# Attention, dense FFN and expert FFN in one kernel: values of eight heads in one part, space of its own for the first expert tile, two gather buffers

## The chip, the cores and the metric

The kernel runs on one core of a Trainium2 chip. The metric is the device time of one execution in microseconds (us). The profile names the engines PE (TensorE), DVE (VectorE), ACT (ScalarE), POOL (GpSimd) and SP (SyncE); PEld is the weight load of PE.

## The reference

Three layers follow each other: a linear attention with complex decay, a dense FFN, and an expert FFN that sends each token to one of eight experts.

```python
# attention: q, k, v, a of [4, 8, 768, 48]; scale a to magnitude <= 0.999
for t in range(S):
    S_re, S_im = ar * S_re - ai * S_im, ar * S_im + ai * S_re
    S_re = S_re + k[t] (x) v[t]
    y[t] = q[t] @ S_re
x = y as [3072, 384]
# dense FFN, 384 -> 2048 -> 384
h = x @ w_in
x = (h * tanh(log1p(exp(h)))) @ w_out
# experts, 8 of 384 -> 1024 -> 384
logits = x @ w_gate + modality_bias[modality_id]
e = argmax(logits); gate = softmax(logits)[e]
out = gate * (relu(x @ w1[e]) @ w2[e])
```

All is float32. The kernel gets float32 accuracy from products of three matmuls on values split into a high and a low half (`xh`/`xl`, `gh`/`gl`, `hhs`/`hls`, `v` in sets of two).

## The kernel before

**Work.** 3072 tokens are cut into 12 units of 256. A unit goes through the attention in two chunks of 128 tokens (`scores`, a mask on DVE, `values` into `py`, the carried state `st`), then through the dense FFN in 8 steps. An h step (`ph`) has 18 matmuls, and its o step (`po`, 12 matmuls) follows three steps later (LAG = 3). The last o step of a unit gives the gate logits; routing sorts the tokens of a half of the sequence into expert tiles: `route 0` for the first half runs during the later units, `route 1` for the second half after the last unit, in some 125 small DVE instructions on the scratch `ar`, whose result is `tt` (which rows to fetch and where to put them). Tiles 0 to 4 hold the first half's tokens, 5 to 11 the second half's, 256 rows each; 12 to 14 are small tiles of 128 rows.

**A tile.** Four loads of 768 KB bring the weights of its expert into `r0s`/`r1s`; ACT writes the high half and DVE the low half (`v`, 128x1536). POOL gathers the rows by an indirect DMA (`xg`), PE transposes them (`pt`), ACT and DVE split them into `y`. Then four steps of `qhs` (18 matmuls) and `qos` (12), again with a lag of three, and a scatter of the results (`out<-oss`, POOL). In a small tile one `qhs` has 9 matmuls of 512 columns.

**What sets the order.** Class `Plan` (L91) collects strands: lists of operations with a due time. `run` lists them out greedily, at each step the operation that can start first by modelled costs, on a tie the one with the earlier due time. What `part()` encloses stays together on one engine; `wait` and `mark` name events, and a mark of kind "order" counts from the issue of the instruction before it. The emitted order is fixed at build time: on each engine instructions run in that order, and semaphores make them wait for data. Nearly all work is recorded through one helper, so that its line in the profile is L261. Class `Line` keeps the PE steps of FFN and tiles in one chain: step n's h matmuls, then the o matmuls of step n-3, or in the other order where `swap` is set. `NoStep` is an empty step in that chain.

**Names that the change touches.** `att_scores` (L541) issues scores, masks and values of a chunk. Each tile gets its transposed rows from `Tile.rows` (L1350), which waits in the strand `gather n` for the routing and for the transposes of the tile before (`tu{n-1}`), because there is one buffer `xr` for the gathered rows. Tile 0's rows `y` lie in the buffers `xh` and `xl` of the dense FFN, and wait for the h matmuls of the last step (`H95`). `g.const` is a pool that lives to the end, `g.stk` a pool of the attention that is freed behind it.

Of the kernel before, what the change touches and what calls it, by code (L numbers as in the profile page):

```python
# [7 lines left out]
F32 = mybir.dt.float32  # L8
F32R = mybir.dt.float32r
I32 = mybir.dt.int32  # L10
# [6 lines left out]
B, H, S, D = 4, 8, 768, 48  # L17
DM = H * D
NT = B * S
DFF = 2048  # L20
E, F2 = 8, 1024
CH = 128
NU = NT // 256
KD = DM // 128
# [260 lines left out]
def setup(g, ins):  # L285
    nc = g.nc
    c = g.const
    g.ident = c.tile([128, 128], F32, name="ident")
    g.mask = c.tile([128, 1, 128], F32, name="mask")
    nc.sync.dma_start(out=g.ident, in_=ins["c_ident"])  # L290
    nc.sync.dma_start(out=g.mask[:, 0, :], in_=ins["c_mask"])
    g.nident = c.tile([128, 128], F32R, name="nident")
    nc.scalar.activation(out=g.nident, in_=g.ident, func=AF.Copy, scale=-1.0)
    nc.scalar.preload_act_table_set("natural_log_exp_and_others")
    for t in g.vt + g.st:
        nc.gpsimd.memset(t[:, :, 48:64], 0.0)
    for t, n in zip(g.scan, (1, 2, 4, 1)):
        nc.gpsimd.memset(t[:, 0, 0:n], 1.0)
        nc.gpsimd.memset(t[:, 1, 0:n], 0.0)
    g.dend = c.tile([128, NU, 6], F32, name="dend")  # L300
    g.asum = c.tile([128, NU + 1], F32, name="asum")
# [239 lines left out]
def att_scores(g, ins, ci, xT):  # L541
    nc, p = g.nc, g.plan
    u, c = divmod(ci, 2)
    cc = ci % 6
    QK, v, s0 = g.QK[u], g.vt[ci % 2], g.st[ci % 2]
    p.wait(f"QK{u}_0")
    py = g.aps.tile([128, 4, 128], F32, tag="py", name=f"py{ci}")
    sc = {}

    def scores(hg):  # L550
        ps = g.aps.tile([128, 4, 128], F32, tag="ps", name=f"ps{ci}_{hg}")
        with p.part():
            for h in range(4):
                nc.tensor.matmul(ps[:, h, :], QK[hg][0:96, h, 1, c, 0:128], QK[hg][0:96, h, 0, c, 0:128], start=True, stop=True)
        return ps

    def mask(hg, ps):
        sc[hg] = g.apw.tile([128, 4, 128], F32, tag="sc", name=f"sc{ci}_{hg}")
        nc.vector.tensor_mul(sc[hg], ps, g.mask.to_broadcast([128, 4, 128]))

    def values(hg):
        with p.part():
            for h in range(4):
                hh = hg * 4 + h
                o = py[(hh % 2) * 64:(hh % 2) * 64 + 64, hh // 2, :]
                nc.tensor.matmul(o, v[:, hh, :], sc[hg][:, h, :], start=True, stop=cc == 0)
                if cc > 0:
                    nc.tensor.matmul(o, s0[:, hh, :], QK[hg][0:96, h, 0, c, 0:128], start=False, stop=True)

    mask(0, scores(0))  # L570
    p.wait(f"QK{u}_1", f"v{ci}")
    ps = scores(1)
    if cc > 0:
        p.wait(f"s{ci - 1}")
    values(0)
    mask(1, ps)
    values(1)
    p.mark(f"y{ci}")
    Y = g.apw.tile([128, 4, 128], F32, tag="sc", name=f"Y{ci}")
    nc.scalar.copy(out=Y, in_=py)  # L580
    dst = xT.rearrange("(p a e) t -> a e p t", a=2, e=48)
    for a in range(2):
        with p.behind(f"x{u}"):
            nc.sync.dma_start(out=dst[a, :, :, ci * 128:(ci + 1) * 128], in_=Y[a * 64:a * 64 + 48])
# [339 lines left out]
def route_setup(g, ctx, ins):  # L924
    nc = g.nc
    c = g.const
    g.iota_e = c.tile([128, 1, E], F32, name="iota_e")
    g.iota_t = c.tile([128, NHALF[1], 1], F32, name="iota_t")
    g.iota_p = c.tile([128, 128], F32, name="iota_p")
    g.ids = c.tile([128, NT // 128, 2], F32, name="ids")  # L930
    g.tri = c.tile([128, 128], F32, name="tri")
    g.ones = c.tile([128, 128], F32, name="ones")
    nc.sync.dma_start(out=g.iota_e[:, 0, :], in_=ins["c_iota_e"])
    nc.sync.dma_start(out=g.iota_t[:, :, 0], in_=ins["c_iota_t"])
    nc.sync.dma_start(out=g.iota_p, in_=ins["c_iota_p"])
    nc.sync.dma_start(out=g.ids, in_=ins["c_ids"])
    nc.sync.dma_start(out=g.tri, in_=ins["c_tri"])
    nc.vector.memset(g.ones, 1.0)
    route_space(g, c)
    g.etab = [c.tile([128, NFM + NSM + 2], I32, name=f"etab{i}") for i in range(2)]  # L940
    g.bias = c.tile([128, NT // 128, E], F32, name="bias")
    mb = c.tile([128, 2, E], F32, name="mb")
    mi = c.tile([128, NT // 128, 2], I32, name="mi")
    nc.sync.dma_start(out=mb, in_=ins["mb"].partition_broadcast(128))
    nc.sync.dma_start(out=mi, in_=ins["mid"].bitcast(I32).rearrange("p (b w) -> p b w", w=2))
    sh = [128, NT // 128, E]
    m0 = c.tile([128, NT // 128], F32, name="m0")
    m1 = g.logit
    V = nc.vector
    V.tensor_scalar(out=m0, in0=mi[:, :, 0], scalar1=0.0, scalar2=None, op0=ALU.is_equal)  # L950
    V.tensor_mul(g.bias, m0.unsqueeze(2).to_broadcast(sh), mb[:, 0:1, :].to_broadcast(sh))
    V.tensor_scalar(out=m0, in0=mi[:, :, 0], scalar1=1.0, scalar2=None, op0=ALU.is_equal)
    V.tensor_mul(m1, m0.unsqueeze(2).to_broadcast(sh), mb[:, 1:2, :].to_broadcast(sh))
    V.tensor_add(g.bias, g.bias, m1)
# [340 lines left out]
class Tile:  # L1295


    def __init__(self, g, ins, n, gi, i, halves, x2, out):
        self.g, self.n, self.gi, self.i, self.halves, self.out = g, n, gi, i, halves, out
        at = 2 * i if halves == 2 else 2 * NFM + i  # L1300
        self.tt = g.tt[gi][:, :, at:at + halves]
        self.w1, self.w2 = g.sets[n % 2]
        self.hs, self.ph, self.po = {}, {}, None
        self.due = due(NU) + min(n, NA + NB) * TSTEP * 4 + max(n - NA - NB, 0) * TSTEP * 1.5
        self.nm = f"s{n}"
        if n == 0:
            self.x = [g.mx.tile([128, KD, 256], F32R, tag=t, name=f"y{t}", bufs=1) for t in ("xh", "xl")]
        else:
            self.x = g.xsets[n % 2]
        self.weights(ins)  # L1310
        self.rows(x2)
# [39 lines left out]
    def rows(self, x2):  # L1351
        g, p, n, tt = self.g, self.g.plan, self.n, self.tt
        nc = p
        nr = NT * (self.gi + 1) // 2
        xg = g.mx.tile([128, 2, DM], F32, tag="xr", name=f"xg{n}", bufs=1)
        pts = []
        with p.strand(f"gather {n}", self.due - 30), p.behind(f"G{n}"):
            p.wait(f"tt{self.gi}", *(f"x2_{b}" for b in range(nr // 128)), f"tu{n - 1}" if n else f"X{NU - 1}")
            for c in range(self.halves):
                p.gpsimd.indirect_dma_start(  # L1360
                    out=xg[:, c], out_offset=None, in_=x2[0:nr, :],
                    in_offset=bass.IndirectOffsetOnAxis(ap=tt[:, 0, c:c + 1].bitcast(U32), axis=0),
                    bounds_check=nr - 1, oob_is_err=False)
        with p.strand(f"turn {n}", self.due - 12):
            p.wait(f"G{n}")
            for c in range(self.halves):
                p.take("pt")
                pt = g.m2.ps.tile([128, KD, 128], F32, tag="pt", name=f"pt{n}_{c}")
                with p.part():
                    for k in range(KD):  # L1370
                        p.tensor.transpose(pt[:, k, :], xg[:, c, k * 128:(k + 1) * 128], g.ident)
                pts.append(pt)
                p.mark(f"pt{n}_{c}")
            p.mark(f"tu{n}")
        xh, xl = self.x
        for c in range(self.halves):
            with p.strand(f"rows {n} {c}", self.due - 11):
                p.wait(f"pt{n}_{c}")
                if n == 0:
                    p.wait(f"H{8 * NU - 1}")  # L1380
                elif n == 1:
                    p.wait(f"O{8 * NU - 5}")
                elif n == 2:
                    p.wait(f"O{8 * NU - 7}")
                if n > 2:
                    p.wait(*self.tiles[n - 2].done(1))
                cs = slice(c * 128, (c + 1) * 128)
                split(g, xh[:, :, cs], xl[:, :, cs], pts[c])
                p.give("pt")
                p.mark(f"Y{n}")  # L1390
# [30 lines left out]
class TileStep:  # L1421
    middle = None

    def __init__(self, tile, j):
        self.t, self.j = tile, j
        self.due = tile.due + j * TSTEP
        self.swap = tile.n == j == 0

    def first(self, line):
        t, j = self.t, self.j  # L1430
# [234 lines left out]
def body(tc, ctx, ins, out):  # L1665
# [34 lines left out]
    moe2_sets(g)  # L1700
    w1 = g.wts.tile([128, WP[1]], F32, tag="w9", name="ar1")
    Tile.tiles = tiles = []
    steps.extend([NoStep] * 2)
    for n in range(NA + NB + NS):
        gi, i, halves = (0, n, 2) if n < NA else (1, n - NA, 2) if n < NA + NB else (1, n - NA - NB, 1)
        tiles.append(Tile(g, ins, n, gi, i, halves, x2, out))
# [101 lines left out]
```

## Time and profile before

| | |
|---|---|
| median of 3 runs | 955.14 us (952.89 to 955.41) |
| profiled execution | 951.5 us, span 949.6 us |
| PE busy | 874.9 us, 92% of the span |
| DVE busy | 732.7 us, 77% |
| ACT busy | 668.8 us, 70% |
| POOL busy | 175.2 us, 18% |

The span is the time from the first to the last instruction of the profiled execution. Busy shares are means over stages: the attention starts up to about 125 us, attention and dense FFN run side by side to about 670, the expert tiles follow up to about 936, and the last scatters end the span. A time in brackets behind a row is how long the engine was idle before it, and the arrow names what ended that.

### The profile page before, as it was taken

Reading aid. Unit: us, or ns where it says so; the run is one execution under the profiler, and the core shown is the slowest. Engines: PE = TensorE matmul, PEld = TensorE weight load, DVE = VectorE, ACT = ScalarE, POOL = GpSimd, SP = SyncE. Lnnn points to the kernel's source line nnn. Section 1 sums busy time; section 2 is a strip of 40 time slices with the busy share of each in tenths; the row PEclk is TensorE's granted clock in tenths of the full one; section 3 lists DMA queues with packets and bytes.
Section 4 is the critical chain, followed back from the end, with each engine's and each line's share of the span. In section 5 each row is a group of like instructions: output and inputs, shape, how many; then the busy total and the mean of one; then the engine's idle time right before and its main releaser. Section 6 shows DMA issues by size and latency. Waiting matters only on the chain.

```text
span 949.6 us, 17369 instructions
## 1 busy us (share of the span) xinstructions
PE 874.9 (92%) x6401; PEld 828.8 (87%) x6401; DVE 732.7 (77%) x1517; ACT 668.8 (70%) x1093; POOL 175.2 (18%) x237
## 2 busy tenths in 40 slices
PE   1489899999999999998999999999899999999993
PEld 1267789999999989998999999999799999999883
DVE  4989788889898988798889899764699865565541
ACT  5786969787968787887788787767754556556551
POOL 1021202112120221030303020202112034332211
PEclk9979899999999999999999999999799999999997
DMA  9923323425252534233524142305654767666730
GB/s 306 347 68 89 96 71 113 112 78 124 78 124 67 135 93 109 68 95 107 134 68 123 46 102 67 93 26 194 225 190 136 247 216 237 218 223 212 235 123 7
DMA packets 102749, 128.22 MB, mean 135 GB/s; under 512 B 34601, under 2 KB 76599, under 8 KB 102656
## 3 DMA queue, kind: packets, MB, share of 16 engines
q1 hardware_dynamic: 89680, 89.00, 31.4%
q0 software_dynamic: 12976, 38.03, 13.3%
q8 instruction: 52, 0.85, 0.4%
q14 instruction: 41, 0.34, 0.1%
HBM read 93.74 MB, written 14.82 MB: 114 GB/s over the span
## 4 chain that ended last, share of the span: by engine, by line
PE 46%; ACT 22%; issue 11%; DMA 9%; DVE 8%; POOL 2%; SPq 0%; ACTq 0%; POOLq 0%; DVEq 0%
PE ph L261 11%; PE po L261 10%; ACT u L261 9%; PE py L261 5%; PE ps L261 5%; DMA out<-oss,tt 5%; PE qhs L261 4%; ACT X L261 3%; ACT S L261 3%; PE pst L261 3%; PE qos L261 3%; PE pl L261 2%; DVE ar L261 1%; ACT gh L261 1%; ACT v L261 1%
## 5 line engine op out<-in xcount | busy, mean ns | idle before, releaser
L261 ACT ACTIVATE u<-u 128x512 f32<-128x512 f32 x384 | 237.8, 629 | 6.5
L261 PE MATMUL po<-wt,gh 128*128 128x392 f32 x768 | 206.7, 350 | 2.3 <-ACT gh L261 2.0
L261 PE MATMUL ph<-xh,wt 128*128 128x256 f32 x1152 | 193.5, 288 | 6.6 <-ACT xh L261 4.1
L261 PEld LDWEIGHTS ph<-xh,wt 128*128 128x128 f32 x1152 | 163.5, 191 | 11.5 <-ACT xh L261 4.8
L261 PEld LDWEIGHTS po<-wt,gh 128*128 128x128 f32 x768 | 135.2, 190 | 6.6 <-issue 2.9
L261 PE MATMUL po<-wt,gl 128*128 128x392 f32 x384 | 132.0, 344 | 2.1 <-DVE gl L261 2.1
L261 PE MATMUL qos<-v,hhs 128*128 128x384 f32 x432 | 111.8, 339 | 0.0
L261 POOL DMA_DIRECT2D QK<-X x120 | 65.6, 554 | 230.7 <-ACT xs L261 72.1
L261 PE MATMUL qhs<-y,v 128*128 128x256 f32 x792 | 103.1, 283 | 0.0
L261 PE MATMUL ph<-xl,wt 128*128 128x256 f32 x576 | 101.5, 285 | 1.6 <-DVE xl L261 1.4
L261 PEld LDWEIGHTS qhs<-y,v 128*128 128x128 f32 x792 | 98.7, 189 | 0.0
L261 DVE TENSOR_TENSOR v<-r1s,v 128x1536 fp32r<-128x1536 f32 x30 | 52.7, 1757 | 49.0 <-ACT v L261 46.1
L261 ACT ACTIVATE u<-ph 128x512 f32<-128x512 f32 x96 | 56.7, 591 | 45.6 <-PE ph L261 41.9
L261 DVE SCALAR_TENSOR_TENSOR u<-u,ph 128x512 f32<-128x512 f32 x96 | 65.5, 683 | 26.3 <-ACT u L261 26.1
L261 PEld LDWEIGHTS ph<-xl,wt 128*128 128x128 f32 x576 | 82.7, 191 | 3.2 <-DVE xl L261 3.1
L261 DVE TENSOR_TENSOR gl<-u,gh 128x512 fp32r<-128x512 f32 x96 | 65.7, 686 | 14.6 <-ACT gh L261 14.5
L261 ACT ACTIVATE gh<-u 128x512 fp32r<-128x512 f32 x96 | 60.1, 627 | 23.7 <-DVE u L261 23.6
L261 PEld LDWEIGHTS po<-wt,gl 128*128 128x128 f32 x384 | 72.9, 190 | 3.5 <-DVE gl L261 3.3
L261 PEld LDWEIGHTS qos<-v,hhs 128*128 128x128 f32 x432 | 75.3, 188 | 0.1
L261 POOL DMA_INDIRECT xg<-x,tt x27 | 42.3, 1568 | 167.5 <-PE pt L261 116.6
L261 PE MATMUL qos<-v,hls 128*128 128x384 f32 x216 | 72.6, 336 | 0.0
L261 ACT ACTIVATE hhs<-qhs 128x512 fp32r<-128x512 f32 x48 | 28.7, 599 | 59.2 <-PE qhs L261 58.2
(149 smaller groups left out, 1598.3 us busy)
## 6 DMA issues: line engine op xcount, KB each, us to landing
r0s<-in_w SPq DMA_DIRECT2D x30, 768.0 KB, 4.5
r1s<-in_w SPq DMA_DIRECT2D x30, 768.0 KB, 4.8
QK<-X POOLq DMA_DIRECT2D x72, 96.8 KB, 3.4
QK<-X SPq DMA_DIRECT2D x72, 96.8 KB, 3.7
r<-in_wo SPq DMA_DIRECT2D x8, 768.0 KB, 7.9
r<-in_wi SPq DMA_DIRECT2D x8, 768.0 KB, 13.5
X<-in_q POOLq DMA_DIRECT2D x12, 384.0 KB, 4.9
A<-in_ai POOLq DMA_DIRECT2D x12, 384.0 KB, 4.5
```

Source lines behind the costliest of these rows:

```text
L261: self.plan.add(self.name, *cost[:2], lambda: real(*a, **k), *cost[2:])
```

## The change

`values` of both groups of four heads are issued in one part, behind both masks. Four small tiles (`mask`, `mb`, `mi`, `m0`) move from the pool that lives to the end to that of the attention. Tile 0's rows get space of their own (`yh`, `yl`) and no longer wait for the last h step; its first `qhs` follows in the usual order of a step, and the two empty steps ahead of it go. The gathered rows lie in two buffers: odd tiles from 3 on take the buffer `xh`, so that gather n waits for the transposes of tile n-2 (gather 3 for the last h step), and an order mark `gg` keeps the gathers in sequence.

```diff
 def att_scores
     mask(0, scores(0))
     p.wait(f"QK{u}_1", f"v{ci}")
-    ps = scores(1)
+    mask(1, scores(1))
     if cc > 0:
         p.wait(f"s{ci - 1}")
-    values(0)
-    mask(1, ps)
-    values(1)
+    with p.part():
+        values(0)
+        values(1)
...
-    g.mask = c.tile([128, 1, 128], F32, name="mask")
+    g.mask = g.stk.tile([128, 1, 128], F32, name="mask")
...
         if n == 0:
-            self.x = [g.mx.tile([128, KD, 256], F32R, tag=t, name=f"y{t}", bufs=1) for t in ("xh", "xl")]
+            self.x = [g.m2.w.tile([128, KD, 256], F32R, name=f"y{t}") for t in "hl"]
...
-        xg = g.mx.tile([128, 2, DM], F32, tag="xr", name=f"xg{n}", bufs=1)
+        xg = g.mx.tile([128, 2, DM], F32, tag="xh" if n > 2 and n % 2 else "xr", name=f"xg{n}", bufs=1)
+        behind = f"H{8 * NU - 1}" if n == 3 else f"tu{n - 2 + (n < 3)}" if n else f"X{NU - 1}"
...
-            p.wait(f"tt{self.gi}", *(f"x2_{b}" for b in range(nr // 128)), f"tu{n - 1}" if n else f"X{NU - 1}")
+            p.wait(f"tt{self.gi}", *(f"x2_{b}" for b in range(nr // 128)), behind, *([f"gg{n - 1}"] if n else []))
...
+            p.mark(f"gg{n}", "order")
...
-                if n == 0:
-                    p.wait(f"H{8 * NU - 1}")
-                elif n == 1:
+                if n == 1:
                     p.wait(f"O{8 * NU - 5}")
...
-        self.swap = tile.n == j == 0
+        self.swap = False
...
-    steps.extend([NoStep] * 2)
```

**In the instruction order, PE at the start of unit 7.** `py_481` are the values of that unit's second chunk, `ph_6` and `ph_7` the last h steps of the unit before; `ph_0` of unit 7 follows behind two more o steps in both. The end of the values before:

```order
L261 MATMUL py_481<-QK_7_464,st_98 64x128
L261 MATMUL py_481<-sc_1_485,vt_96 64x128
L261 MATMUL py_481<-QK_7_464,st_98 64x128
L261 MATMUL ph_7_892<-xh_858,wt_252 128x256 x3
L261 MATMUL ph_7_892<-xl_859,wt_252 128x256 x3
L261 MATMUL ph_7_892<-xh_858,wt_252 128x256 x3
L261 MATMUL po_0_878<-wt_217,gh_4_883 128x392 x2
```

With the change the last rows of `py` and what stands next to them:

```order
L261 MATMUL py_481<-QK_7_464,st_98 64x128
L261 MATMUL py_481<-sc_1_485,vt_96 64x128
L261 MATMUL py_481<-QK_7_464,st_98 64x128
L261 MATMUL ph_6_888<-xh_858,wt_239 128x256 x3
L261 MATMUL ph_6_888<-xl_859,wt_239 128x256 x3
L261 MATMUL ph_6_888<-xh_858,wt_239 128x256 x3
L261 MATMUL po_0_878<-wt_204,gh_3_877 128x392 x2
```

The values have moved from the middle of `ph_7` into `ph_6`: half an h step, an o step and half an h step stand between more than before.

**PE at the change of stage.** `po` with `wt_230` is o step 5 of the last unit, `wt_243` o step 6; `pt_0` and `pt_1` are transposes of tile 1's rows. Before:

```order
L261 MATMUL po_1_1074<-wt_230,gh_5_7513 128x392 x2
L261 MATMUL po_1_1074<-wt_230,gl_5_7512 128x392
L261 MATMUL pt_0_7413<-ident,xg_7412 128x128 x3
L261 MATMUL pt_1_7414<-ident,xg_7412 128x128 x3
L261 MATMUL po_0_1073<-wt_243,gh_6_7517 128x392 x2
L261 MATMUL po_0_1073<-wt_243,gl_6_7516 128x392
```

With the change, from the end of o step 4 (`wt_217`):

```order
L261 MATMUL po_1_1074<-wt_217,gl_4_1077 128x392
L261 MATMUL qhs_0_7522<-yh,v_0_7378 128x256 x3
L261 MATMUL qhs_0_7522<-yl,v_0_7378 128x256 x3
L261 MATMUL qhs_0_7522<-yh,v_2_7380 128x256 x3
L261 MATMUL qhs_0_7522<-yh,v_0_7378 128x256 x3
L261 MATMUL qhs_0_7522<-yl,v_0_7378 128x256 x3
L261 MATMUL qhs_0_7522<-yh,v_2_7380 128x256 x3
L261 MATMUL po_0_1073<-wt_230,gh_5_7513 128x392 x2
```

`qhs_0` of tile 0 stands between o steps 4 and 5 now, and `qhs_1` to `qhs_3` in the same way behind 5, 6 and 7.

**POOL at the last tiles.** `xg_7489`, `xg_7495` and `xg_7501` are the gathers of tiles 12, 13 and 14; the `out` rows come in pairs, one pair to a tile of 256 rows. Before:

```order
L261 DMA out<-oss_0_7675,tt_618 3072x384
L261 DMA out<-oss_1_7676,tt_618 3072x384
L261 DMA xg_7489<-x_61,tt_618 128x384
L261 DMA out<-oss_0_7691,tt_618 3072x384
L261 DMA out<-oss_1_7692,tt_618 3072x384
L261 DMA xg_7495<-x_61,tt_618 128x384
L261 DMA out<-oss_0_7707,tt_618 3072x384
L261 DMA out<-oss_1_7708,tt_618 3072x384
L261 DMA xg_7501<-x_61,tt_618 128x384
L261 DMA out<-oss_0_7726,tt_618 3072x384
```

With the change:

```order
L261 DMA xg_7489<-x_61,tt_618 128x384
L261 DMA out<-oss_0_7675,tt_618 3072x384
L261 DMA out<-oss_1_7676,tt_618 3072x384
L261 DMA xg_7495<-x_61,tt_618 128x384
L261 DMA out<-oss_0_7691,tt_618 3072x384
L261 DMA out<-oss_1_7692,tt_618 3072x384
L261 DMA xg_7501<-x_61,tt_618 128x384
L261 DMA out<-oss_0_7707,tt_618 3072x384
L261 DMA out<-oss_1_7708,tt_618 3072x384
L261 DMA out<-oss_0_7726,tt_618 3072x384
```

Each gather stands one pair of scatters further ahead.

## Rows read from the trace of the kernel before

**Rows 1.** Windows: start:end, length, busy us (instructions) by engine, PEclk, DMA share, GB/s.

```profile
0.00:75.00 75.00, 39.69 (x185) 28.78 (x185) 57.60 (x104) 54.10 (x90) 10.08 (x31) 0.91 0.67 229
125.00:650.00 525.00, 514.93 (x4034) 493.27 (x4034) 445.35 (x1032) 411.98 (x726) 83.38 (x140) 1.00 0.36 98
440.00:450.00 10.00, 7.52 (x45) 7.23 (x46) 8.18 (x11) 9.90 (x15) 0.00 (x0) 0.83 0.30 90
676.00:684.00 8.00, 5.85 (x18) 4.81 (x18) 5.18 (x7) 4.29 (x6) 0.25 (x1) 0.50 0.91 325
684.00:759.30 75.30, 75.15 (x552) 74.84 (x552) 67.95 (x171) 38.52 (x45) 11.25 (x10) 1.00 0.61 192
700.00:895.00 195.00, 193.90 (x1396) 192.88 (x1395) 135.09 (x220) 108.06 (x131) 56.08 (x41) 1.00 0.67 213
```

**Rows 2.** Timeline of PE, starts of units 5 and 7: start, us, operation [idle before].

```profile
334.05 0.44 PE L261 MATMUL py<-QK,st 96*64 96x128 f32 x4
...
343.54 0.62 PE L261 MATMUL ph<-xh,wt 128*128 128x256 f32 x3 [1.36 <-ACT xh L261]
...
433.52 0.44 PE L261 MATMUL py<-QK,st 96*64 96x128 f32 x4
...
442.26 0.92 PE L261 MATMUL ph<-xh,wt 128*128 128x256 f32 x3 [2.75 <-ACT xh L261]
```

**Rows 3.** Timeline of PE, end of the last unit and start of tile 0.

```profile
667.97 0.52 PE L261 MATMUL po<-wt,gh 128*128 128x392 f32 x2
...
671.74 0.63 PE L261 MATMUL po<-wt,gh 128*128 128x392 f32 x2 [0.72 <-ACT gh L261]
673.62 0.45 PE L261 MATMUL po<-wt,gl 128*128 128x392 f32 x1 [1.25 <-DVE gl L261]
...
677.84 1.02 PE L261 MATMUL po<-wt,gh 128*128 128x392 f32 x2 [1.30 <-ACT gh L261]
679.72 0.69 PE L261 MATMUL po<-wt,gl 128*128 128x392 f32 x1 [0.85 <-DVE gl L261]
...
692.49 0.52 PE L261 MATMUL qos<-v,hhs 128*128 128x384 f32 x2
```

**Rows 4.** Timeline of ACT in the same stretch.

```profile
677.71 1.48 ACT L261 ACTIVATE v<-r1s 128x1536 fp32r<-128x1536 f32 x1
...
688.37 0.60 ACT L261 ACTIVATE hhs<-qhs 128x512 fp32r<-128x512 f32 x1 [1.56 <-PE qhs L261]
```

**Rows 5.** Tile 5: DVE's group of hls before tt, then timelines of DVE, POOL, PE.

```profile
L261 DVE SCALAR_TENSOR_TENSOR hls<-qhs,hhs 128x512 fp32r<-128x512 f32 x17 | 11.6, 685 | 1.7 <-ACT hhs L261 1.7
...
759.26 0.20 DVE L261 CAST tt<-tb 128x38 int32<-128x38 f32 x1 [1.26 <-PE tb L261]
...
759.58 1.75 DVE L261 TENSOR_TENSOR v<-r1s,v 128x1536 fp32r<-128x1536 f32 x1
...
759.73 2.52 POOL L261 DMA_INDIRECT xg<-x,tt  x1 [7.27 <-DVE tt L261]
...
766.55 1.03 PE L261 MATMUL pt<-ident,xg 128*128 128x128 f32 x6 [0.95 <-DMA xg<-x,tt]
...
772.69 2.28 PE L261 MATMUL qhs<-y,v 128*128 128x256 f32 x18
```

**Rows 6.** Tile 14: timeline of POOL, then of PE.

```profile
887.41 1.05 POOL L261 DMA_INDIRECT xg<-x,tt  x1 [8.58 <-PE pt L261]
...
895.42 0.98 POOL L261 DMA_INDIRECT out<-oss,tt  x1 [3.18 <-ACT y L261]
896.71 2.18 POOL L261 DMA_INDIRECT xg<-x,tt  x1 [0.30 <-issue]
...
903.52 0.88 PE L261 MATMUL pt<-ident,xg 128*128 128x128 f32 x3 [3.43 <-DMA xg<-x,tt]
904.05 3.50 PE L261 MATMUL qhs<-v,y 128*128 128x512 f32 x9
...
909.93 2.25 PE L261 MATMUL qhs<-v,y 128*128 128x512 f32 x9
```

More of the change, by code (lines that the diff above doesn't have):

```diff
@@ L561, in values @@
     def values(hg):
[L562 to L568, printed above, removed]
+        for h in range(4):
+            hh = hg * 4 + h
+            o = py[(hh % 2) * 64:(hh % 2) * 64 + 64, hh // 2, :]
+            nc.tensor.matmul(o, v[:, hh, :], sc[hg][:, h, :], start=True, stop=cc == 0)
+            if cc > 0:
+                nc.tensor.matmul(o, s0[:, hh, :], QK[hg][0:96, h, 0, c, 0:128], start=False, stop=True)
     mask(0, scores(0))
     p.wait(f"QK{u}_1", f"v{ci}")
-    ps = scores(1)
+    mask(1, scores(1))
     if cc > 0:
         p.wait(f"s{ci - 1}")
-    values(0)
-    mask(1, ps)
-    values(1)
+    with p.part():
+        values(0)
+        values(1)
     p.mark(f"y{ci}")
@@ L941, in route_setup @@
     g.bias = c.tile([128, NT // 128, E], F32, name="bias")
-    mb = c.tile([128, 2, E], F32, name="mb")
-    mi = c.tile([128, NT // 128, 2], I32, name="mi")
+    mb = g.stk.tile([128, 2, E], F32, name="mb")
+    mi = g.stk.tile([128, NT // 128, 2], I32, name="mi")
     nc.sync.dma_start(out=mb, in_=ins["mb"].partition_broadcast(128))
@@ L946, in route_setup @@
     sh = [128, NT // 128, E]
-    m0 = c.tile([128, NT // 128], F32, name="m0")
+    m0 = g.stk.tile([128, NT // 128], F32, name="m0")
     m1 = g.logit
```

## The prediction

> **What bounds the kernel now.** I read the table of windows first [rows 1]. From 125 to 650 us TensorE (PE) is busy in 514.93 of 525 us, from 700 to 895 in 193.90 of 195, both at the full granted clock: there only fewer or shorter pauses of PE can shorten the kernel, and a pause saved ahead of 700 us reaches the end. PE is idle at the start (39.69 of 75 us busy), at the change from the dense FFN to the expert tiles around 676, and behind its last matmul, where the change moves nothing. So I looked next at PE's timeline for every wait over 0.2 us: four places stay, and the change touches each.
>
> First, starts of units [rows 2]. A unit's first h step needs the attention output of its tokens, which goes through a copy on ScalarE, two DMAs and a split. At unit 7 the last `py` ends at 433.96 and the first `ph` begins at 442.26, 8.3 us later, 2.75 of them a wait; at unit 5 it is 334.49 to 343.54, 9.05 us, with 1.36 of wait. After unit 7's wait the granted clock of 440 to 450 is 0.83 [rows 1], between the levels of 1.2 and 2.4 GHz: of 7.52 busy us some 17% or 1.3 us are lost. Second, the change of stage [rows 3]: o steps 6 and 7 of the last unit wait 0.72, 1.25, 1.30 and 0.85 us, 4.12 together, and the clock is 0.50 between 676 and 684. Third, tile 5: its gather starts when the routing of the second half is done (`tt` at 759.26), and its transposes wait 0.95 us for `xg` [rows 5]. Fourth, tile 14: its transposes wait 3.43 us for `xg`, and then comes a `qhs` group of 3.50 us where the next takes 2.25 [rows 6].
>
> **Values of eight heads in one part.** The 8 or 16 small matmuls no longer stand in two places. Work is the same. They stand behind both masks now, and the scheduler, which gives a part to PE without a gap, places the last `py` elsewhere between the steps. A step of 18 `qhs` matmuls takes 2.28 us [rows 5]; an o step has 12 of 392 columns, 2% more columns in all; I count 2.2 for each kind. By the order of before, 3.5 steps stood between the last `py` and the first `ph` of unit 5 (7.7 us) and 2.5 at unit 7 (5.5 us), against a chain of 8.3 to 9.05: short by 1.4 and 2.8 to 3.5, as the waits say. All other units had 4.5 steps (9.9 us) or more and no wait. By the order of after it is 4 steps (8.8) at units 2, 5 and 8, 3.75 (8.2) at 11, and 4.5 or more at all others, 7 among them. Removed: 1.36 + 2.75 + 1.3 = 5.4 us. Added: 8.7 (middle of the two chains) less the cover is 0 at 2, 5 and 8 and 0.5 at 11; with the longer chain 0.25 three times and 0.85, with half a clock loss 1.4 in the middle. Taken: -4.0; bounds -5.4 (no new wait) and 0 (chain at its longest and a clock loss of 1.3 at three of the four places, 1.6 + 3.9 = 5.5). The wait for the second mask costs PE nothing as long as a step stands between; the order keeps one there. The start, 0 to 75 us, is ordered a little differently as well: PE is no bound there (39.69 busy) and DVE with 57.60 does the same work: 0, bounds -3 and +3, about the size of one unit-start wait.
>
> **Tile 0 with its own space.** Before, tile 0's rows took the `xh` and `xl` buffers of the last unit, so its first step came after all of that unit's h steps and two empty steps kept the lag. Now `qhs` 0 to 3 stand between o steps 4 to 7. PE's work from the start of o step 5 at 667.97 to the first `qos` at 692.49 [rows 3] is the same: three o steps (6.6), four `qhs` groups (9.1), six transposes (1.0), 16.7 of 24.5 us at the full clock. At most 7.8 us can go. What is late next is ScalarE: `gh` of step 7 came at 677.84, and now two `hhs` (0.60 each) and one `v` (1.48) more stand ahead of it [rows 4], 2.7 us: 680.5. From there o step 7 and `qhs` 3 take 4.4 us, so `qos` starts at 684.9: -7.6. Lower bound -7.8; upper -3, if `gh` comes later by two more splits (3.0) and PE's clock falls again. The moves of the mask and bias tiles to another pool issue the same DMAs: nothing.
>
> **Tile 5 behind it.** PE now reaches tile 5 7.6 us earlier, 772.69 - 7.6 = 765.1. Its rows come from `tt`: `tt` 759.26, transposes 766.55, hence 7.3 us, then 2.7 for the transposes and the two splits: `tt` + 10. DVE works through `tt`'s small operations among weight splits; from 684 to 759.3 it is busy 67.95 of 75.30 us [rows 1]. In the new order 14 instead of 17 `hls` of 685 ns stand ahead of it, -2.1 us; its start is 1 us later (a split more ahead); of 7.35 us of idle time between none or half goes. `tt` falls between 758.2 and 754.5, and tile 5 between 768.2 and 764.5, a loss of 3.1 or of 0. I take +1.0. If the routing is no faster at all it is 769.3, +4.2.
>
> The descriptor instruction of that gather takes 2.52 us beside a `v` split on DVE that runs from 759.58 to 761.33 [rows 5], while the scatter's at 895.42, with no such split, takes 0.98 [rows 6]. The Trainium skill (SBUF — State Buffer, section "SBUF: two separate sides") states that GpSimd is locked out of the port it shares with DVE, and cannot write descriptors, while DVE runs a two-port operation. The trace agrees at this place: the instruction ends 0.9 us after the split. By that rule, an estimate, an earlier gather gains or loses up to 1.5 us by what DVE does just then; by the rows alone I add nothing for it.
>
> **Two gather buffers.** A gather of tile n now waits for the transposes of tile n-2. Only two gathers are late in the trace, those of tiles 5 and 14; the others have landed when PE comes, so their earlier start is worth nothing. Tile 14's was issued at 896.71, behind the `out` scatter of 895.42 [rows 6], and PE waited 3.43 us. Its new condition, the transposes of tile 12, was met when tile 13's gather was issued at 887.41, and it stands ahead of that scatter pair now, so up to 9.3 us earlier: it lands near 894, when PE wants it near 900. -3.43, and -1.25 for the slow group after it: -4.7. Bounds: -5.1 (the three transposes too, 0.88 us where six took 1.03 [rows 5]) and 0 (the gather late still, held by what is queued ahead on POOL). What is queued behind these gathers on POOL are scatters of tiles done, for which nobody waits but the last one; that one is unchanged, and so is the tail after PE's end. The further wait that tile 0's rows lose (for the last h step) is in the 7.6.
>
> **Sum.** -4.0 - 7.6 + 1.0 - 4.7 = -15.3 us. The profiled execution took 951.5 us (span 949.6 and 1.9 around it): 936.2. It was 3.6 us faster than the median of the runs shown, 955.14, so the median after is 955.1 - 15.3 = 939.8; I say 940.
>
> **Rivals.**
> (A) The second routing sets tile 5. DVE, not PE, is then the bound from 684 to 769: the whole of what the change of stage gives but 3.4 us is given back as a wait of `pt` for `xg` at tile 5. For it: DVE's 67.95 of 75.30 us. Against: three `hls` less, and idle time that can go. -4.0 - 7.6 + 4.2 - 4.7 = -12.1, 943; with `tt` 3 us later still, 946.
> (B) The unit starts gain nothing: the chain is longer than 9 us at units with 4 steps of cover, or the start loses 3 us. For it: four units are within 0.9 us of the chain. Against: units with 9.9 us did not wait. -11.3 to -8.3, 944 to 947.
> (C) Slower. The chain from the last `py` to `xh` grows at most units, for one cause: the values wait for both masks and the state, so the copy behind them lands among other ScalarE work, 2 us later or more. Each hit costs what unit 7 cost, 2.75 + 1.3 = 4.05 us. The rest gains 11.3, the two old hits return, so with three more hits the gain is gone (12.2), and with six more it is 955.1 - 11.3 + 24.3 = 968. For it: the new covers lie between 8.2 and 9.9, nearer to the chain than most of before. Against: the chain was 8.3 to 9.05 where it could be read, and one wait on a mask (beside a 2.2 us step) is short.
> (D) It doesn't do what it says: `qhs` 0 to 3 stand early but wait for the `v` splits of tile 0, which now compete with the last unit's `gh` and `gl`, and PE waits in another place, at half clock, for as long as before. The stage's change then gives 0. With unit starts and tail as forecast that is -8.7, 946; with the tail's gather late still 951, and with the unit starts at their upper bound too 955, no change.
>
> **How the numbers follow.** Forecast 0.52 (its own range 935 to 944), A 0.18 (943 to 946), B 0.13 (944 to 947), D 0.09 (946 to 955, 0.04 of it above 952.2), C 0.08 (from four hits, 960). A measurement of this kernel tells about 0.3%, 2.9 us, from no change. Faster: 0.52 + 0.18 + 0.13 + 0.05 = 0.88; same 0.04; slower 0.08. The range 932 to 950 leaves out C, the worse half of D and a little below: 2 in 10 at most. Its low end is -23, which takes every lower bound (-5.4, -3 at the start, -7.8, 0, -5.1: -21.3) and 1.5 for the run.
>
> **What would show it.** Values: no wait over 0.6 us of `ph` on `xh` at unit starts but at 2, 5, 8 or 11; wrong if units with 4.5 steps wait over 1 us. Transition: first `qos` near 685 less what the units saved, clock above 0.9 from 670 on, and under 1.5 us of waits. Tile 5: `pt<-ident,xg` waits under 1 us and `tt` lies some 70 us behind the last `logit`; if that wait is 3 us or more it is A. Tail: no wait on `xg` in the last small tile and `qhs` at 2.25 us. The prediction is wrong if PE shows a wait on something that was on no row of before: above all on `v`, `y` or `sc`.

## The result: 932.5 us, 22 us faster, at the lower end of the range

The changed kernel takes 932.53 us (930.52 to 933.15, 4 runs) against 954.62 us for the kernel before (952.89 to 955.41, 4 runs): ratio 0.977, 95% interval 0.975 to 0.979. The forecast was 940, range 932 to 950. A second comparison (5 and 11 runs) gave 0.980 (0.977 to 0.983), 930.65 against 950.50. The gain is 20 to 22 us, not 15: the direction and the size of three of the four terms were right, the first term was too small by half.

The windows of the changed kernel answer to [rows 1]; columns as there.

```profile
125.00:650.00 525.00, 514.38 (x4096) 497.71 (x4095) 447.26 (x1034) 416.33 (x733) 83.77 (x141) 1.00 0.36 98
650.00:700.00 50.00, 48.73 (x342) 48.14 (x343) 44.07 (x92) 36.88 (x49) 11.99 (x10) 1.00 0.73 243
```

The first row is the one to read: PE is as busy between 125 and 650 us as before (514.38 against 514.93), yet it gets through 4096 records of matmuls instead of 4034 (both traces have the same 6401 in all). So the time was not gained from pauses. In the second row, the change of stage now runs at the full granted clock.

To see where the time went I read, for each run, when a certain matmul starts: the first `ph` of units 1 and 11, the first, the 529th and the last `qos`. They are taken from counts of matmuls up to a time, in steps of 0.5 us, so that a difference of 0.5 says nothing. Length of each stretch in us, one profiled execution each:

```
                              start to  unit 1 to  unit 11 to  first to    529th to
                              unit 1    unit 11    first qos   529th qos   last qos
before                         155.0     477.5       60.0       201.5       41.0
changed                        153.5     469.5       53.5       202.0       36.5
values alone                   151.5     470.5       61.0       206.0       42.0
all but values                 155.5     477.5       53.0       202.0       36.5
own space alone                152.5     479.5       53.0       204.5       36.5
two gather buffers alone       154.5     478.0       59.5       200.0       36.5
changed, extra score           154.5     479.5       53.5       202.5       36.5
changed, extra value           151.5     475.5       53.0       202.5       36.5
changed, scores earlier        158.0     467.5       53.0       202.5       36.0
changed, one gather buffer     154.5     470.0       53.0       205.5       37.0
changed, again                 151.0     468.5       53.5       202.5       36.0
changed, one buffer, again     151.0     469.0       53.5       204.0       36.5
changed, later units earlier   154.5     467.0       53.5       202.5       36.5
```

The first column differs by 2.5 us between two executions of the same changed kernel, so nothing is concluded from it.

### The profile page after: what moved, and what is told of

Its sections match the earlier page's. It is cut to its first block, busy times and chain, and to the rows that moved or that the text cites. A ratio compares the mean times of both kernels' runs of the same rounds, so it can differ in the third digit from the quotient of the medians.

```text
span 928.7 us, 17351 instructions
## 1 busy us (share of the span) xinstructions
PE 859.2 (93%) x6401; PEld 820.7 (88%) x6401; DVE 731.6 (79%) x1517; ACT 668.1 (72%) x1093; POOL 167.5 (18%) x237
## 4 chain that ended last, share of the span: by engine, by line
PE 41%; ACT 27%; DVE 17%; DMA 7%; issue 5%; SPq 0%; POOL 0%; ACTq 0%; DVEq 0%; POOLq 0%
ACT u L261 11%; PE qhs L261 8%; PE ph L261 8%; PE qos L261 7%; PE po L261 7%; ACT S L261 4%; ACT X L261 3%; DMA xT<-Y 3%; PE ps L261 3%; DVE S L261 3%; DMA out<-oss,tt 3%; DVE ar L261 3%; PE py L261 2%; DVE v L261 2%; ACT gh L261 2%
## 5 line engine op out<-in xcount | busy, mean ns | idle before, releaser
L261 PE MATMUL po<-wt,gh 128*128 128x392 f32 x768 | 204.3, 347 | 0.3 <-ACT gh L261 0.3
L261 PEld LDWEIGHTS ph<-xh,wt 128*128 128x128 f32 x1152 | 161.6, 189 | 11.8 <-ACT xh L261 4.9
L261 DVE TENSOR_TENSOR v<-r0s,v 128x1536 fp32r<-128x1536 f32 x30 | 52.7, 1756 | 13.7 <-ACT v L261 13.7
```

The costliest lines, as they stand in the source:

```text
L261: self.plan.add(self.name, *cost[:2], lambda: real(*a, **k), *cost[2:])
```

## The experiments

**Each part alone.** The first four kernels are cut from the diff that stands ahead of the prediction, with nothing else edited, but that in the kernel with two gather buffers alone tile 3's gather waits for tile 0's last `qhs`:

```diff
+        behind = "TH0_3" if n == 3 else f"tu{n - 2 + (n < 3)}" if n else f"X{NU - 1}"
```

Values alone: 

> The kernel before with the values of eight heads in one part and nothing else. Between the starts of units 3 and 11 the two traces differ by 7.5 us, the pauses of PE by only 0.9 and the clock by 1.3. Theory 1 (runs): PE pays some 0.3 us whenever its small matmuls change kind, and there is one run of py less in each of 24 chunks; the edit alone gives 24 x 0.3 = 7.5 us and some 1.5 us at the first units, -9 us (ratio 0.990 to 0.991). Theory 2 (the forecast): the edit is worth only the waits at the unit starts, -4 us (0.996), and the rest comes from the other edits.

Measured: 945.19 against 951.47 us, ratio 0.993 (0.990 to 0.996). The median, 6.3 us under before, lies between the two theories; the stretches decide. From unit 1 to unit 11 it is 7 us shorter, nearly the whole of the changed kernel's 8, and at the first `qos` it stood some 10 us ahead (3.5 of them from the start); then it lost 5. PE's waits of over 0.3 us on gathered rows in it:

```profile
756.43 0.55 PE L261 MATMUL pt<-ident,xg 128*128 128x128 f32 x3 [0.78 <-DMA xg<-x,tt]
...
759.90 0.55 PE L261 MATMUL pt<-ident,xg 128*128 128x128 f32 x3 [2.92 <-DMA xg<-x,tt]
...
887.15 0.55 PE L261 MATMUL pt<-ident,xg 128*128 128x128 f32 x3 [0.35 <-DMA xg<-x,tt]
...
898.34 0.87 PE L261 MATMUL pt<-ident,xg 128*128 128x128 f32 x3 [3.28 <-DMA xg<-x,tt]
```

That is 7.3 us on `xg` at tiles 5, 13 and 14, where before had 4.4 [rows 5, 6]. Most of what is lost is at tile 5, and it is not the one buffer: both of its gathers start when `tt` is there. The second descriptor instruction began while DVE ran a split, and took 2.45 us:

```profile
752.41 1.76 DVE L261 TENSOR_TENSOR v<-r0s,v 128x1536 fp32r<-128x1536 f32 x1 [0.42 <-ACT v L261]
```

```profile
752.61 2.45 POOL L261 DMA_INDIRECT xg<-x,tt  x1 [0.31 <-issue]
```

In the kernel before, the same instruction began ahead of that split, and took 1.02 us:

```profile
762.55 1.02 POOL L261 DMA_INDIRECT xg<-x,tt  x1 [0.31 <-issue]
```

```profile
763.08 1.76 DVE L261 TENSOR_TENSOR v<-r0s,v 128x1536 fp32r<-128x1536 f32 x1 [1.15 <-ACT v L261]
```

Its rows landed 7.25 us behind its start instead of 4.43, hence the wait of 2.92 us, and behind that wait the granted clock was 0.5 for 3.4 us. The instruction began 0.2 us behind the start of the split; had it begun ahead of it, as before, the wait would have been short. I call that chance.

All but values: 

> The changed kernel with the values in two parts again, all else changed. Theory 1: -22.1 + 9 = -13 us against the kernel before (0.986). Theory 2: -18 us (0.981).

Measured: 940.57, ratio 0.990 (0.986 to 0.993), 10.9 us under before; unit 1 to unit 11 is 477.5, as before, and after unit 11 the stretches are those of the changed kernel to 0.5 us. Both theories expected a larger gain of the rest, since both took it from the first comparison's 22.1 us. The three other terms of the forecast, -7.6 + 1.0 - 4.7, make -11.3, which is what this kernel shows. The 8 us between the units belong to the values: theory 2 is out.

Own space alone: 

> The kernel before with tile 0's own space, the pool moves and no empty steps; one gather buffer, values as before. Both theories: the first qos of tile 0 some 7 us earlier; tile 14's transposes still wait for xg. If tile 5 is gated by the second routing (rival A) the wait there is 3 us or more and the kernel gains 3 us; if not, it waits about 1 to 1.5 us as in the changed kernel and gains 5.5 to 7 us (0.993 to 0.994).

Measured: 943.26, ratio 0.993 (0.990 to 0.996). The change of stage is 7 us shorter, and tile 5 waits 1.1 us for `xg`, so rival A, which asked for 3 us or more there, is out. The stretch behind it is 3 us longer all the same (204.5 against 201.5): a matmul of the routing (`tb`) waits 1.42 us for DVE's `ar`, and tile 13's transposes wait 1.50 us for `xg`. That tile 14 would still wait was wrong: the last stretch is 36.5 too. With the empty steps gone, tile 14's transposes come 5.2 us behind the issue of their gather, where PE wanted them 3.4 us behind it before (903.52 - 3.43 - 896.71, [rows 6]). The gather was also quicker: its descriptor instruction took 1.04 us instead of 2.18, with no split of DVE under way when it began, and the rows landed 4.5 us behind its start instead of 6.7. At 6.7 us PE would still have waited. POOL and PE of that kernel:

```profile
890.42 1.04 POOL L261 DMA_INDIRECT xg<-x,tt  x1 [0.30 <-issue]
```

```profile
895.64 0.49 PE L261 MATMUL pt<-ident,xg 128*128 128x128 f32 x3
```

Two gather buffers alone: 

> The kernel before with two gather buffers and nothing else (tile 3's gather waits for tile 0's last qhs, since its buffer holds tile 0's rows). Forecast: only tile 14's wait goes, -4.7 us (0.995). If the landing time of the gathers had cost nothing: 0.

Measured: 946.42, ratio 0.995 (0.993 to 0.998), 5.1 us against the 4.7 of the forecast, and the last stretch is 4.5 us shorter. Tile 5's wait of 0.95 us is gone in this trace too, which was not expected. So either of two parts takes away tile 14's wait; together they take it away once.

**What a change of kind costs PE.** Two kernels add one matmul to each chunk of the changed kernel at the same place, with a modelled cost of 0, so that the order of everything else stays:

```diff
         values(0)
+        p.call("tensor", 0.0, 0.2, lambda: p.real.tensor.matmul(py[:, 2, :], QK[1][0:96, 0, 1, c, 0:128], QK[1][0:96, 0, 0, c, 0:128], start=True, stop=True))
         values(1)
```

Extra score, as above: 

> The changed kernel with one more matmul in each chunk, of the kind of the scores (K and Q, 96 rows, 128 columns out), put between the values of the two groups of heads into a place of py that the next values write over. Nothing else moves. The matmul itself is 2 records of 0.10 us, 24 x 0.2 = 4.8 us. Theory 1 (a change of kind costs PE 0.25 us or so, py to ps and back): 24 x (0.2 + 0.25 to 0.35), 11 to 13 us over the changed kernel. Rival (no cost of a change of kind; the fewer runs of py helped in another way): 5 us over it.

Extra value (`py[0:64, 2, :], v[:, 4, :], sc[1][:, 0, :]` in its place): 

> The same place, but the extra matmul is of the kind of the values (a repetition of the next one): 2 records of 0.055 us, 24 x 0.11 = 2.6 us over the changed kernel by both theories. The difference to the run with the extra score is 2.2 us for the matmul itself, and by theory 1 6 to 8 us more.

Measured: 944.02 and 937.09 us, ratios 0.991 (0.988 to 0.995) and 0.984 (0.980 to 0.987): 6.9 us between the medians, where the rival has 2.2 and theory 1 8 to 10. It is nearer to theory 1, and under it. The trace shows it directly. PE's rows around the extra score, the line L576:

```profile
326.21 0.44 PE L261 MATMUL py<-QK,st 96*64 96x128 f32 x4
326.57 0.49 PE L576 MATMUL py<-QK 96*128 96x128 f32 x2
326.99 0.45 PE L261 MATMUL py<-sc,vt 128*64 128x128 f32 x4
```

and around the extra value:

```profile
323.02 0.44 PE L261 MATMUL py<-QK,st 96*64 96x128 f32 x4
323.24 0.38 PE L576 MATMUL py<-sc,vt 128*64 128x128 f32 x2
323.46 0.44 PE L261 MATMUL py<-sc,vt 128*64 128x128 f32 x4
```

From the start of the four before it to the start of the four behind it: 0.78 us with the score, 0.44 with the value. Four records of `py` among themselves take 0.22. A score group's eight records take 0.81 with what comes behind, so two of them 0.20 at most, and the two changes of kind cost at least 0.78 - 0.22 - 0.20 = 0.36, near 0.2 each.

The extra value itself was mis-sized. Its two records take 0.22 us (323.24 to 323.46), as long as four of `py` elsewhere, and not 0.11: 24 of them are 5.3 us and not 2.6. It writes the same half of `py` as the matmul behind it, where the heads alternate between the two halves; that this is the reason is not shown. So matmul for matmul the two extras take the same time, 0.20 and 0.22 us, and a rival without a cost of a change has about nothing for the difference between them, not 2.2.

The whole run of values takes 2.58 and 2.18 us, 0.40 apart, in 17 of the 20 chunks from unit 1 to unit 11. That is 6.8; the stretch shows only 4.0. Of the rest 1.7 us are shorter waits of PE in the kernel with the extra score, above all of the later `ph` for `xl` (longer runs are also longer cover); about 1 us is not accounted for.

**More cover at the unit starts.** The due time of the scores, 4 us earlier for all units, then from unit 4 on:

```diff
-            with p.strand(f"scores {ci}", due(u) - 43 + 6 * c):
+            with p.strand(f"scores {ci}", due(u) - (47 if u >= 4 else 43) + 6 * c):
```

All units (47 everywhere): 

> The changed kernel with the scores of each chunk due 4 us earlier, which puts the values some steps further ahead of the next unit: work between the last py and the first ph of a unit 8.6 us at unit 5 and 9.7 or more elsewhere (8.1 to 9.7 in the changed kernel). Theory A: the waits of ph for xh and xl (7.2 us over eleven units in the changed kernel) are what the cover lacks; they fall under 2.5 us and the kernel gains 4 to 5 us. Theory B: they come from the split of x itself, whatever the cover, and nothing changes.

Measured: 933.87, ratio 0.980 (0.977 to 0.984). Unit 1 to 11 is 2 us shorter, and the waits for `xh` and `xl` between 125 and 650 us fall from 5.9 to 3.0 us. The first stretch is 4.5 us longer in this one execution, more than the 2.5 us by which it scatters. Theory A holds for the mechanism, with half the size; that the start takes it back is likely, and not shown.

From unit 4 on: 

> The changed kernel with the scores due 4 us earlier from unit 4 on, and units 0 to 3 left as they are. Where all units were shifted, the stretch from unit 1 to unit 11 was 2 us shorter and the waits for xh and xl half as long, but the start 4.5 us later. Work between last py and first ph is 9.7 us or more from unit 3 on here. If the start was only the shift of the first units: 2 to 3 us faster than the changed kernel (0.974 to 0.975 of before). If the loss at the start and the gain belong together: the same as the changed kernel.

Measured: 929.84 against 930.65 for the changed kernel beside it, 0.978 (0.975 to 0.981) and 0.980 (0.977 to 0.983). The waits, from 155 to 620 us (total, times, longest), of the changed kernel:

```profile
PE ph L261 <- DVE xl L261: 3.4, 9, 0.5
PE ph L261 <- ACT xh L261: 1.9, 3, 0.6
```

and of this one:

```profile
PE pst L261 <- ACT KT L261: 2.7, 4, 0.8
...
PE ph L261 <- DVE xl L261: 1.5, 4, 0.4
PE ph L261 <- ACT xh L261: 1.2, 2, 0.6
PE py L261 <- DVE sc L261: 1.2, 1, 1.2
```

2.6 us of waits for `xh` and `xl` go and 1.9 of `pkt` for `KT`, and `pst` and `py` wait 3.9 us, against 0.3 in the changed kernel. It is the fastest median here, but no measurable gain over the changed kernel.

**One gather buffer in the changed kernel.** The two lines of the gather are put back, with nothing else.

First time: 

> The changed kernel with one gather buffer, as before. By the run with the values alone, which was 10 us ahead at the end of the dense FFN and 4.9 at the end of the program, the one buffer costs more the earlier PE comes: four waits for xg of 7.3 us there. Expected 7 to 9 us over the changed kernel. If the two buffers save the same as alone (4.5 to 7.5 us), there is no such interplay.

Measured: 933.77, ratio 0.979 (0.975 to 0.984), without the changed kernel beside it: inconclusive.

Second time: 

> The changed kernel with one gather buffer, a second time, now beside the changed kernel itself: its times went from 928.5 to 938.2. Theory A: two buffers are worth 4 to 5 us in the changed kernel too, as alone (0.982 of before against 0.977). Theory B: they are worth nothing once the rest is changed (both within 0.3%).

The changed kernel beside it: 

> The changed kernel as it is, to stand beside the next two on the same chip. Both theories: 0.977 of before.

Measured: 933.44 (0.984, interval 0.980 to 0.988) against 930.65 (0.980, 0.977 to 0.983). 2.8 us, between both theories, and the intervals overlap. The stretches have it at the tiles, 1.5 and 3 us in the two pairs nearest in time; the last stretch is the same within 0.5. Between the first and the 529th `qos` PE waits 3.8 us in this kernel and 1.9 in the changed one beside it: `tb` 1.43 us for `ar` instead of 0.18, and tile 13's transposes 1.53 us for `xg` instead of nothing, while tile 5 waits 0.81 instead of 1.71. In the changed kernel the second buffer is worth some 2 to 3 us, not 4.7, and I do not call that measured.

## Why the prediction was right, and where it was not

The four terms, read from the stretches, are -8.0, -6.5, +0.5 and -4.5, together -18.5, against -4.0, -7.6, +1.0 and -4.7; the start gives 1.5 us more in this pair of executions.

**The values were mis-sized: this is the step that failed.** The forecast said "Work is the same" of the values, priced them by waits at the unit starts alone, and took -4.0. From unit 1 to 11 it is -8.0, beyond the term's own bounds of -5.4 and 0. That the whole still fell into the range is in part luck: its low end had allowances for the start and the run. The trace of before held the answer. Here is one chunk of it; read the starts in the left column, from the first row of a group of small matmuls to the FFN row behind it: `ps`, then `ps` with `py`, then `py`.

```profile
317.24 1.06 PE L261 MATMUL ps<-QK 96*128 96x128 f32 x8
318.05 0.60 PE L261 MATMUL po<-wt,gh 128*128 128x392 f32 x2
...
320.27 1.05 PE L261 MATMUL ps<-QK 96*128 96x128 f32 x8
321.25 0.45 PE L261 MATMUL py<-sc,vt 128*64 128x128 f32 x4
...
322.33 0.63 PE L261 MATMUL ph<-xh,wt 128*128 128x256 f32 x3
...
324.69 0.45 PE L261 MATMUL py<-sc,vt 128*64 128x128 f32 x4
...
325.77 0.63 PE L261 MATMUL po<-wt,gh 128*128 128x392 f32 x2
```

The same chunk with the change, `ps`, `ps`, `py`:

```profile
315.08 1.05 PE L261 MATMUL ps<-QK 96*128 96x128 f32 x8
315.89 0.60 PE L261 MATMUL po<-wt,gh 128*128 128x392 f32 x2
...
318.11 1.05 PE L261 MATMUL ps<-QK 96*128 96x128 f32 x8
318.92 0.59 PE L261 MATMUL ph<-xh,wt 128*128 128x256 f32 x3
...
321.24 0.45 PE L261 MATMUL py<-sc,vt 128*64 128x128 f32 x4
...
322.18 0.44 PE L261 MATMUL py<-sc,vt 128*64 128x128 f32 x4
322.40 0.44 PE L261 MATMUL py<-QK,st 96*64 96x128 f32 x4
322.62 0.44 PE L261 MATMUL py<-sc,vt 128*64 128x128 f32 x4
...
323.21 0.62 PE L261 MATMUL po<-wt,gh 128*128 128x392 f32 x2
```

PE is away from FFN steps for 0.81 + 2.06 + 1.08 = 3.95 us before and for 0.81 + 0.81 + 1.97 = 3.59 now, with the same matmuls: 0.36 a chunk. Between units 1 and 11 lie 20 chunks, three of them with half the records of `py`; added up over all of them, PE is away for 76.3 us before and 69.6 now. That is 6.7 of the 8.0; the rest is about the lost clock at unit 7 (1.3) and 0.35 us of shorter pauses. Where `py` follows `ps` directly, its start comes 0.98 us after that of `ps`, where an FFN step comes after 0.81; a run of `py` less also saves one way in and one way out. The order has nearly as many visits of `ps` and `py` as before (72 against 73), but 24 runs of `py` instead of 48.

**The unit starts gave almost nothing.** Of the 5.4 us of waits and lost clock that were to go, the waits on `xh` and `xl` between 125 and 650 us did not fall at all (5.5 us before, 5.9 now, in more and shorter ones); only the 1.3 us of clock at unit 7 went. PE's waits there (total, times, longest), before:

```profile
PE ph L261 <- ACT xh L261: 4.1, 2, 2.7
...
PE ph L261 <- DVE xl L261: 1.4, 5, 0.5
```

and with the change:

```profile
PE ph L261 <- DVE xl L261: 4.0, 10, 0.6
...
PE ph L261 <- ACT xh L261: 1.9, 3, 0.6
```

Units 7 and 5 of the changed kernel answer to [rows 2]:

```profile
424.27 0.44 PE L261 MATMUL py<-QK,st 96*64 96x128 f32 x4
...
434.54 0.62 PE L261 MATMUL ph<-xh,wt 128*128 128x256 f32 x3
435.53 0.62 PE L261 MATMUL ph<-xl,wt 128*128 128x256 f32 x3 [0.37 <-DVE xl L261]
```

```profile
339.84 0.62 PE L261 MATMUL ph<-xh,wt 128*128 128x256 f32 x3 [0.63 <-ACT xh L261]
340.83 0.62 PE L261 MATMUL ph<-xl,wt 128*128 128x256 f32 x3 [0.37 <-DVE xl L261]
```

At unit 7 the cover of 9.8 us (424.71 to 434.54) is enough for `xh`, but the second half of the split comes later, and 0.4 us of wait appears at nearly every unit. The forecast had counted the chain to `xh` alone and called 4.5 steps safe. For `xh` it was right: PE waits for it at units 2, 5 and 8 alone, 0.63 us each, three of the four units that it named. What it left out is `xl`, though PE waited for `xl` at five unit starts in the trace of before as well; its list of every wait over 0.2 us passed over these, and over some 4 us of `pkt` and `pst` on `KT`, which the change does not move. Rival C asked for a chain to `xh` that outgrows the cover at most units; that did not come. A hit on `xl` at most units did, at 0.4 to 1.0 us together with `xh` where C has 4 us, and none of these waits took the clock down: the changed kernel's trace has no granted clock under 1.00 between 125 and 650 us.

**The change of stage was right**: -6.5 against -7.6. The rows answer to [rows 3].

```profile
659.42 0.51 PE L261 MATMUL qhs<-yh,v 128*128 128x256 f32 x3
...
671.26 0.63 PE L261 MATMUL po<-wt,gh 128*128 128x392 f32 x2 [0.29 <-ACT gh L261]
...
672.12 0.45 PE L261 MATMUL po<-wt,gl 128*128 128x392 f32 x1 [0.24 <-DVE gl L261]
...
676.17 0.59 PE L261 MATMUL qos<-v,hhs 128*128 128x384 f32 x2
```

From the 4.12 us of waits 0.53 stay, on the same two operands, and from 650 to 700 us the granted clock is 1.00; rival D is out.

**Tile 5 was right in size, by luck**: +0.5 against +1.0. DVE, POOL and PE answer to [rows 5]:

```profile
745.21 0.20 DVE L261 CAST tt<-tb 128x38 int32<-128x38 f32 x1 [0.75 <-PE tb L261]
...
746.74 1.76 DVE L261 TENSOR_TENSOR v<-r0s,v 128x1536 fp32r<-128x1536 f32 x1 [0.52 <-ACT v L261]
```

```profile
745.68 1.04 POOL L261 DMA_INDIRECT xg<-x,tt  x1 [7.62 <-DVE tt L261]
747.03 2.36 POOL L261 DMA_INDIRECT xg<-x,tt  x1 [0.31 <-issue]
```

```profile
755.64 0.55 PE L261 MATMUL pt<-ident,xg 128*128 128x128 f32 x3 [0.27 <-DVE y L261]
...
757.77 2.04 PE L261 MATMUL qhs<-y,v 128*128 128x256 f32 x15 [1.21 <-DVE y L261]
```

`tt` comes 69 us behind the first `qos` where it was 67 before, and nobody waits for `xg`. The forecast's loss was to come from late rows, and there is none; in its place PE waits 1.21 us for `y`, which was in no term. The forecast itself had named a wait on `y` as a sign that it is wrong, and here it was. It also held the second buffer worthless here; with one buffer this stretch is 1.5 to 3 us longer.

The descriptor instruction takes 1.04 us where it begins ahead of the split on DVE and 2.36 where it begins beside it (746.74 to 748.50), ending 0.9 us after it. The forecast said that the scatter of 0.98 us at 895.42 had no split beside it; one began at 896.22, before that scatter ended. What these rows tell apart is which begins first: in the two traces, before and with the change, all 35 gathers and scatters that begin 0.05 us or more into a split end 0.85 to 0.92 us behind it, and the 19 in which a split begins under way take 0.97 to 1.11 us. The Trainium skill (SBUF — State Buffer, section "SBUF: two separate sides") says that an operation of DVE in a two-port mode, or one with two SBUF inputs against an operation of GpSimd that reads SBUF, holds the shared pair of ports for the whole instruction if it starts first, and that the other then blocks. The split has two SBUF inputs, and the gathers and scatters take their row numbers from the tile `tt`, so this would be the second case, not the two-port operation that the forecast named. The rows agree in one direction only: a split that begins beside a running descriptor instruction is no longer than the others (1.76 us at 763.08 in the kernel before).

**The tail was right in size, for one reason too few**: -4.5 against -4.7, but the own space alone gives it as well (there with a gather that happened to be quicker). The forecast looked only at POOL's queue and not at where tile 14's transposes move on PE. Such terms do not add: the three parts alone give -6.3, -8.2 and -5.1 by their medians, 19.6 together, near the 19.9 to 22.1 of the whole, and yet the tail's 4.5 is in two of them and the values alone lose 5, most of it at tile 5, that they keep in the whole.

## What to carry to other kernels

Count how often PE changes between kinds of small matmuls, not only how many there are: in the trace, take the time from the first of them to the next large one, and compare runs of one kind with runs of two. A chain that ends in a split has two ends; measure the cover against the later one. And when two edits remove the same wait, price it once, but look at what a gain upstream makes late.

## What was not expected of the hardware

A change between the score kind (96 rows, 128 columns) and the value kind (64 columns) costs PE near 0.2 us at the full granted clock, and so does a way in and out of a run of `py` among FFN steps (1.08 us for 16 records, 1.97 for 32, so 0.19 less for one run than for two). The trace puts it on no wait: it counts as busy PE. A change of rows alone is not it: within a run the records go from 128 rows to 96 and back every four, with starts 0.22 us apart for each four (322.18, 322.40, 322.62), and single records start 0.053 us apart across such a change and 0.056 without one. Why the other change costs time is open: the runs do not tell the 128 columns of a score from the two halves of 64 in which the values are written.
